# Block convolution of an S4 and SwiGLU stack: one sum of each unit as an accumulating transfer, and the kernel's first spectra read from DRAM

## The chip, the cores and the metric

The kernel runs on one core of one Trainium2 chip. The metric is device time in microseconds (us) of one execution; the runs of the kernel before gave 1077.13, 1077.5 and 1078.07, median 1077.5. Lower is better.

Engines are named as in the profile: PE is TensorE (matmuls), DVE is VectorE, ACT is ScalarE, POOL is GpSimd and SP is SyncE, which issues most transfers. Each engine works through its own list of instructions in order, and so does each issuing queue.

## The reference, cut to what matters

The input `x` has one batch, 2048 positions and 512 channels. Two layers are applied with the same weights; each is a long convolution along the positions (S4), then a SwiGLU block, both with a layernorm ahead and a residual behind.

```python
K = jnp.einsum("dn,dnl,dn->dl", Cc, P, dB).real        # kernel of 2048 taps per channel
Kf = rfft2(pad(K));  Uf = rfft2(pad(u))                # zero-padded to 4096
y = irfft2(Uf * Kf)[:L] + u * Dskip                    # causal convolution
...
x = x + _A_ref(_layernorm(x), ...)                     # convolution
x = x + (silu(n @ w_gate) * (n @ w_up)) @ w_down       # SwiGLU, n = _layernorm(x), F = 1376
```

All of it is float32 in and out.

## The kernel before

**Blocks and pairs.** The 2048 positions are cut into four blocks of 512. A pair is (layer, block); the eight pairs are done in the order `SEQ = ((0,0),(0,1),(0,2),(1,0),(0,3),(1,1),(1,2),(1,3))`. For each pair there is a convolution (`ssm`) and a feed-forward part (`ffn`). The main loop emits the convolution of pair i+1 ahead of the feed-forward part of pair i, so that the two run beside each other.

**Convolution of a block.** A 512-position block is turned into spectra by matmuls with DFT tables (`forward`, PE line L284, results taken by ACT and DVE). The output block b is the inverse transform of a sum over k = 0..b of (spectrum of kernel block k) times (spectrum of input block b−k). It is done in eight *units* a pair: two halves h of the channels, four residues q of the frequencies (`s` counts them). Per unit and k, DVE makes one product of 128x1024 float32 (L817: all four real and imaginary combinations at once, into `yk` for k = 0, else into `t`) and for each k > 0 one sum `yk += t` (L820). Two small rows (L825, L826, 128x256) then fold `yk` into a complex result, further sums (L772, L773, L838 to L850) make the four inputs of the inverse transform, and PE does the inverse (`pi`, L789), six matmuls of 128x256 for each.

The kernel's spectra are in DRAM (`wdr`, blocks k = 1 to 3), and those of k = 0 stay in SBUF for the whole run (`w0r`, 16 KB a partition). A product with k > 0 loads its two factors by SP: `w` (L813) and `uu` (L815), 256 KB each, three buffers of each kind. `yk` and `t` have one buffer each.

**Feed-forward part.** It is done in two halves of 256 positions a pair, 16 in all. In each half PE makes six groups of gate and up products in PSUM, `pgu`, which has two buffers: five whole groups (L935, L936, L938, 48 matmuls each) and one *remainder* of 96 columns (L904 to L906), which comes first. ACT takes the gate through Silu (L941), DVE multiplies with the up product (`sg`, L942; L913 for the remainder), ACT and DVE split the result in two float16 parts (`hh` L943, `hl` L944), and PE multiplies these with `w_down` (`py`, L951 to L953, 66 matmuls of 128x512). A group of PE can start only when DVE's `sg` row of the group two before it has read its buffer. Weights and activations are split in high and low float16 parts, which is why every product has three matmuls.

**What sets the order.** Until about 340 us the order is written out by hand. From there a scheduler places the instructions of all engines by priority: feed-forward rows on ACT and DVE, and the DFT matmuls, carry a high priority (`BOOST`), convolution rows on DVE carry none. The scheduler's order is fixed when the kernel is built: on the chip an engine doesn't overtake a row that waits.

**POOL** has little work here: it stores spectra to DRAM (`udr`, L744), and makes the inverse square roots of the norms (`rs`, L231), on which the next half's input depends.

Of the kernel before, what the change touches and what calls it, by code (L numbers as in the profile page):

```python
# [11 lines left out]
F32 = mybir.dt.float32  # L12
# [4 lines left out]
OP = mybir.AluOpType  # L17
# [5 lines left out]
P = 128  # L23
# [9 lines left out]
DC = 64  # L33
# [44 lines left out]
def kernel(ctx, tc, x, a_re, a_im, b_re, b_im, c_re, c_im, log_dt, d_skip,  # L78
# [7 lines left out]


    BUFS = dict(ga=1, gb=1, n=1, bt=1, z=1, u=3, y1=1, uu=3, w=3, t=1, bd=2, t1=3,
                xf=1, nn=1, hh=1, hl=1, sg=1, hf=1, stats=2, stats2=2, ef=1)

    def tl(shape, name, tag, dt=F32):
        return sb.tile(shape, dt, name=name, tag=tag, bufs=BUFS[tag])
# [40 lines left out]
    w0r = sb.tile([P, 2, 4, NQ, 2, DC], F32, name="w0r")  # L133
# [620 lines left out]
    def ssm_half(layer, b, h):  # L754
        first = layer == 0 and b == 0
        half = SEQ.index((layer, b)) >= INV
        hs = slice(h * HD, (h + 1) * HD)
        free = iv[h] if first else iv[0]

        def slot():  # L760
            return free.pop(0) if free else tl([P, 2, HD], "yf", "w")

        def done(t):
            if any(t is o for o in ivs):
                free.append(t)
        if half and not yl2:
            yl2.append(tl([P, 2, 2, 2, HD], "yl2", "hf", F16))

        def add_sub(x, y):

            t = slot()
            V.tensor_tensor(t, x, y, OP.add)  # L772
            V.tensor_tensor(x, x, y, OP.subtract)  # L773
            done(y)
            return t, x

        def inverse(pi, r, v):

            if half:
                yl = yl2[0][:, r % 2]  # L780
                A.activation(yl[:, 0], v, AF.Copy, scale=sy[:, 0:1])
                stt(yl[:, 1], v, sy[:, 0:1], yl[:, 0], OP.subtract)
            with tc.high_priority(offset=0 if first else BOOST):
                if half:
                    terms = [(eih[:, r, i, le], yl[:, ly, i]) for i in range(2) for le, ly in ((0, 0), (0, 1), (1, 0))]
                else:
                    terms = [(ei[:, r, i], v[:, i]) for i in range(2)]
                for k, (e, o) in enumerate(terms):
                    PE.matmul(pi[:, r % 2], lhsT=e, rhs=o, start=k == 0, stop=k == len(terms) - 1)  # L789
# [12 lines left out]
        for s in range(4):  # L802
            hq, q, u = ahead.pop(0)
            nxt = next(spec, None)
            if nxt:
                ahead.append(nxt)
            yk = tl([P, NQ, 2, 2, DC], "yk", "y1")
            for k in range(b + 1):
                if k == 0:
                    w, uu = w0r[:, h, q], spectrum(u) if any(u is o for o in fss) else u  # L810
                else:
                    w = tl([P, NQ, 2, DC], "w", "w")
                    nc.sync.dma_start(w, wdr[k, h, q])  # L813
                    uu = tl([P, NQ, 2, DC], "uu", "uu")
                    nc.sync.dma_start(uu, udr[layer][b - k, h, q])  # L815
                t = tl([P, NQ, 2, 2, DC], "t", "t") if k else yk
                V.tensor_tensor(t, uu.unsqueeze(2).to_broadcast([P, NQ, 2, 2, DC]),  # L817
                                w.unsqueeze(3).to_broadcast([P, NQ, 2, 2, DC]), OP.mult)
                if k:
                    V.tensor_tensor(yk, yk, t, OP.add)  # L820
            if any(u is o for o in fss):
                fs.append(u)
            y = slot()
            yo = whole(y)
            V.tensor_tensor(yo[:, 0], yk[:, :, 0, 0], yk[:, :, 1, 1], OP.subtract)  # L825
            V.tensor_tensor(yo[:, 1], yk[:, :, 0, 1], yk[:, :, 1, 0], OP.add)  # L826
# [24 lines left out]
        done(d_)  # L851
        inverse(pj, 3, b_)
        result(pi, 0)
        yield
        result(pj, 2)
        yield
# [123 lines left out]
    with tc.manual_schedule(engines={mybir.EngineType.Activation, mybir.EngineType.DVE, mybir.EngineType.PE, mybir.EngineType.Pool}):  # L980
# [168 lines left out]


        c, kts = NCH - 1, (kt2[:, 0], kt2[:, 1])
        xs, eh, yl2 = [None] * 3, [], []
# [159 lines left out]
```

## Time and profile before

| | us |
|---|---|
| median of three runs | 1077.5 |
| the profiled execution, time | 1077.3 |
| the profiled execution, span from first to last instruction | 1075.0 |
| PE busy, DVE busy, ACT busy, POOL busy | 1015.1, 966.5, 544.4, 103.9 |
| the 96 sums L820, the 96 products into `t` L817 | 117.5, 117.5 |

Around the span lie 2.3 us. In the views, "busy" of an engine is the share of a stretch in which at least one instruction was in flight, "mean ns" the length of one instruction. Instructions of one engine overlap a little at their ends, so the step from one start to the next is what an instruction costs a full engine. A matmul record of 128x256 is 0.27 us long while the next one starts 0.11 us later.

A row of a timeline or a chain gives the start, the length, the engine and line, output and inputs; in brackets stands idle time before it and what ended it ("0.55 <-DVE sg L942").

### The profile page before, as it was taken

Reading aid. Unit: us, or ns where it says so; the run is one execution under the profiler, and the core shown is the slowest. Engines: PE = TensorE matmul, PEld = TensorE weight load, DVE = VectorE, ACT = ScalarE, POOL = GpSimd, SP = SyncE. Lnnn points to the kernel's source line nnn. Section 1 sums busy time; section 2 is a strip of 40 time slices with the busy share of each in tenths; the row PEclk is TensorE's granted clock in tenths of the full one; section 3 lists DMA queues with packets and bytes.
Section 4 is the critical chain, followed back from the end, with each engine's and each line's share of the span. In section 5 each row is a group of like instructions: output and inputs, shape, how many; then the busy total and the mean of one; then the engine's idle time right before and its main releaser. Section 6 shows DMA issues by size and latency. Waiting matters only on the chain.

```text
span 1075.0 us, 22004 instructions
## 1 busy us (share of the span) xinstructions
PE 1015.1 (94%) x8918; PEld 801.8 (75%) x8918; DVE 966.5 (90%) x1405; ACT 544.4 (51%) x1093; POOL 103.9 (10%) x163
## 2 busy tenths in 40 slices
PE   1979999998789999999999999999999999999998
PEld 0868888887677787777868677786868677696774
DVE  8999999999999999999999999999999999983221
ACT  6979888853268264366652235523525442144210
POOL 1112222210000001011000001101000000000000
PEclk9989999998899999999999999999999999999999
DMA  5266777878665444323054463442444244413000
GB/s 215 100 177 180 171 165 182 188 187 270 218 207 160 122 130 151 128 94 70 16 138 140 126 212 112 124 133 100 123 120 121 86 122 139 126 36 64 1 26 20
DMA packets 120104, 139.74 MB, mean 130 GB/s; under 512 B 50609, under 2 KB 75697, under 8 KB 119234
## 3 DMA queue, kind: packets, MB, share of 16 engines
q1 hardware_dynamic: 108098, 112.83, 34.9%
q0 software_dynamic: 11904, 25.50, 10.2%
q8 instruction: 70, 1.15, 0.5%
q14 instruction: 32, 0.26, 0.1%
HBM read 91.36 MB, written 30.67 MB: 114 GB/s over the span
## 4 chain that ended last, share of the span: by engine, by line
DVE 37%; PE 27%; issue 4%; DMA 3%; ACT 3%; POOL 1%; DVEq 0%; SPq 0%; ACTq 0%; POOLq 0%
DVE t L817 5%; PE pgu L938 5%; PE pgu L935 5%; PE pgu L936 5%; DVE yk L820 5%; DVE yk L817 4%; PE py L951 3%; PE py L952 3%; PE py L953 3%; DVE sg L942 2%; DVE yl L236 2%; DVE hl L944 2%; DMA st<-in_B_w_down_dram 1%; PE pi L789 1%; PE pw L550 1%
## 5 line engine op out<-in xcount | busy, mean ns | idle before, releaser
L935 PE MATMUL pgu<-mix,wall 128*128 128x256 f16 x1280 | 299.0, 273 | 5.8 <-DVE sy L629 2.1
L936 PE MATMUL pgu<-mix,wall 128*128 128x256 f16 x1280 | 298.9, 273 | 0.0
L938 PE MATMUL pgu<-mix,wall 128*128 128x256 f16 x1280 | 195.7, 273 | 0.0
L936 PEld LDWEIGHTS <-wall 128*128 128x128 f16 x1280 | 125.2, 98 | 22.6 <-issue 7.0
L935 PEld LDWEIGHTS <-wall 128*128 128x128 f16 x1280 | 125.2, 98 | 16.4 <-issue 0.9
L938 PEld LDWEIGHTS <-wall 128*128 128x128 f16 x1280 | 125.2, 98 | 14.6
L951 PE MATMUL py<-wall,hh 128*128 128x512 f16 (+1 forms) x352 | 133.4, 379 | 0.0
L952 PE MATMUL py<-wall,hh 128*128 128x512 f16 (+1 forms) x352 | 133.4, 379 | 0.0
L953 PE MATMUL py<-wall,hl 128*128 128x512 f16 (+1 forms) x352 | 132.2, 379 | 0.0
L820 DVE TENSOR_TENSOR yk<-yk,t 128x1024 f32<-128x1024 f32 x96 | 117.5, 1224 | 0.5
L817 DVE TENSOR_TENSOR t<-uu,w 128x1024 f32<-128x1024 f32 x96 | 117.5, 1224 | 0.2
L943 ACT ACTIVATE hh<-sg 128x512 f16<-128x512 f32 x80 | 50.2, 627 | 117.4 <-DVE sg L942 117.3
L942 DVE SCALAR_TENSOR_TENSOR sg<-pgu,sc,sg 128x512 f32<-128x512 f32 x80 | 60.0, 750 | 39.2 <-ACT sg L941 39.2
L550 PE MATMUL pw<-kt,ek 128*128 128x256 f32 (+1 forms) x384 | 93.4, 381 | 0.0
L941 ACT ACTIVATE sg<-pgu,sc 128x512 f32<-128x512 f32 x80 | 54.3, 678 | 75.1 <-PE pgu L938 62.1
L550 PEld LDWEIGHTS pw<-kt,ek 128*128 128x128 f32 x384 | 75.0, 199 | 8.4
L944 DVE TENSOR_TENSOR hl<-sg,hh 128x512 f16<-128x512 f32 x80 | 55.3, 691 | 8.7 <-ACT hh L943 8.6
L953 PEld LDWEIGHTS <-hl 128*128 128x128 f16 (+1 forms) x352 | 34.3, 98 | 38.0
L952 PEld LDWEIGHTS <-hh 128*128 128x128 f16 (+1 forms) x352 | 34.4, 98 | 37.7
L951 PEld LDWEIGHTS <-hh 128*128 128x128 f16 (+1 forms) x352 | 34.4, 98 | 37.3
L515 PE MATMUL pk<-wall,g 128*32 128x64 f32 x1024 | 57.4, 288 | 4.9 <-DMA g<-g 3.7
L516 PE MATMUL pk<-wall,g 128*32 128x64 f32 x1024 | 57.8, 287 | 0.7 <-issue 0.7
(276 smaller groups left out, 1930.6 us busy)
## 6 DMA issues: line engine op xcount, KB each, us to landing
uu<-udr SPq DMA_DIRECT2D x96, 256.0 KB, 3.0
w<-wdr SPq DMA_DIRECT2D x96, 256.0 KB, 2.7
g<-g POOLq DMA_DIRECT2D x6, 1024.0 KB, 9.1
udr<-fu POOLq DMA_DIRECT2D x22, 256.0 KB, 3.2
udr<-u SPq DMA_DIRECT2D x16, 256.0 KB, 3.3
kdr<-ks SPq DMA_DIRECT2D x6, 512.0 KB, 3.1
kt<-kdr SPq DMA_DIRECT2D x24, 128.0 KB, 3.0
out_dram<-xg SPq DMA_DIRECT2D x12, 256.0 KB, 2.3
```

What stands on the lines that cost most here:

```text
L516: PE.matmul(o, lhsT=g[:, 1, :, d], rhs=im[:, 0:64, d], start=False, stop=True, tile_position=(0, 32 * grp))
L550: PE.matmul(pw[:, i], lhsT=e, rhs=kt[:, :, c + 4 * k0:4 * k1:4, :].rearrange("p g k d -> p k g d"), start=c == 0, stop=c == 3)
L817: V.tensor_tensor(t, uu.unsqueeze(2).to_broadcast([P, NQ, 2, 2, DC]), w.unsqueeze(3).to_broadcast([P, NQ, 2, 2, DC]), OP.mult)
L820: V.tensor_tensor(yk, yk, t, OP.add)
L935: PE.matmul(o, lhsT=wgu(wi, k, 0)[:, fs], rhs=nh[:, k], start=k == 0, stop=False)
L936: PE.matmul(o, lhsT=wgu(wi, k, 1)[:, fs], rhs=nh[:, k], start=False, stop=False)
L938: PE.matmul(o, lhsT=wgu(wi, k, 0)[:, fs], rhs=nlo[:, k], start=False, stop=k == 3)
L942: V.scalar_tensor_tensor(sg, pgu[:, 1], sc6[:, 4:5], sg, OP.mult, OP.mult)
L944: V.tensor_tensor(hl[:, f0:f0 + 2], sg, hh[:, f0:f0 + 2], OP.subtract)
L951: PE.matmul(py[r], lhsT=hh[:n, f, rc], rhs=wd(f, 0)[:n], start=f == 0, stop=False)
L952: PE.matmul(py[r], lhsT=hh[:n, f, rc], rhs=wd(f, 1)[:n], start=False, stop=False)
L953: PE.matmul(py[r], lhsT=hl[:n, f, rc], rhs=wd(f, 0)[:n], start=False, stop=f == FT - 1)
```

## The change

From the fourth pair of `SEQ` on (`APART = 3`), two things differ.

1. **Spectra.** When the fourth pair's convolution is emitted, the spectra of k = 0 are stored from `w0r` to `wdr[0]` (one store of 2 MB, SP). From then on a product with k = 0 loads its factor `w` by SP as the others do. The 16 KB a partition of `w0r` become four more buffers of 4 KB: two for `yk`, two for `t`, three of each in all, used in turn.
2. **The sum for k = 1.** In a unit with b > 0 the product of k = 1 is no longer added by DVE: POOL issues a transfer from `t` to `yk`, within SBUF, which accumulates (128x1024 float32, 512 KB). The products of k = 2 and 3 are added to one another on DVE, and their sum to `yk`. So a unit has one DVE sum less; the very last unit of the run keeps the old form. That makes 31 transfers: eight in each of the pairs (0,3), (1,1), (1,2), seven in (1,3). The fourth pair itself, (1,0), has b = 0 and no sum at all.

```diff
+APART = 3
+        apart = SEQ.index((layer, b)) >= APART
+        if apart and not more:
+            nc.sync.dma_start(wdr[0]..., w0r...)
+            m = tl([P, 4, NQ, 2, 2, DC], "more", "w0r")
+            more.extend(itertools.cycle(o) for o in ((None, m[:, 0], m[:, 1]), (None, m[:, 2], m[:, 3])))
+            def factors(k):
+                if k == 0 and not apart:
+                    return w0r[:, h, q], spectrum(u) if any(u is o for o in fss) else u
+                w = tl([P, NQ, 2, DC], "w", "w")
+                nc.sync.dma_start(w, wdr[k, h, q])
...
+            yk = ybuf()
+            product(yk, 0)
+            behind = apart and b > 0 and not ((layer, b) == SEQ[-1] and h == 1 and s == 3)
+            if behind:
+                t = tbuf()
+                product(t, 1)
+                G.dma_start(flat(yk), flat(t), accum_op=OP.add)
+            t = None
+            for k in range(2 if behind else 1, b + 1):
+                o = tbuf()
+                product(o, k)
+                if behind and t is not None:
+                    V.tensor_tensor(t, t, o, OP.add)
+                elif behind:
+                    t = o
                 else:
+                    V.tensor_tensor(yk, yk, o, OP.add)
+            if t is not None:
+                V.tensor_tensor(yk, yk, t, OP.add)
```

In the changed kernel the product is L840, the sums are L855 and L861, the transfer is L849, the folding rows are L866 and L867, the `sg` rows L983 and (remainder) L954, the `hl` row L985, the store L772, the loads `w` and `uu` L831 and L835; `more` is the tile with the four new buffers. Up to the convolution of the fourth pair the lists of PE and DVE are the same as before; behind it the scheduler has placed everything anew.

**SP's list, at about 275 us.** The store is emitted with the fourth pair, but the scheduler has it much earlier, in the hand-ordered stage. `udr` and `uu` are input spectra, `wall` and `st` pieces of the feed-forward weights. Before:

```order
L320 DMA udr_114<-u 128x512
L815 DMA uu<-udr_114 128x512
L671 DMA wall<-in_B_w_gate_dram 128x4x344
L813 DMA w<-wdr 128x512 x2
L671 DMA wall<-in_B_w_up_dram 128x4x344
L813 DMA w<-wdr 128x512
L697 DMA st_2982<-in_B_w_down_dram 128x4x512
```

Now:

```order
L321 DMA udr_114<-u 128x512
L772 DMA wdr<-w0r 128x8x512
L835 DMA uu<-udr_114 128x512
L672 DMA wall<-in_B_w_gate_dram 128x4x344
L831 DMA w<-wdr 128x512 x2
L672 DMA wall<-in_B_w_up_dram 128x4x344
L831 DMA w<-wdr 128x512
L698 DMA st_2982<-in_B_w_down_dram 128x4x512
```

One row is new, the store, ahead of three loads of spectra and three of weights.

**DVE's list, from the tenth remainder to the first whole group behind it.** This is the second half of the feed-forward part of pair (0,3); beside it run convolution units of pair (1,2). `sg` rows belong to the feed-forward part, `nn`, `nt` and `xf` to norms and residual; rows of 128x1024 are products (with `w`) and sums of the convolution. Before, from one `sg` row to the next:

```order
L913 SCALAR_TENSOR_TENSOR sg_3015<-pgu,sc_92,sg_3015 128x192
L236 SCALAR_TENSOR_TENSOR fbt<-pf,fbt 128x512
L890 TENSOR_TENSOR nn_2990<-nn_2990,nt_2991 128x512
L817 TENSOR_TENSOR t<-uu,w 128x1024
L236 SCALAR_TENSOR_TENSOR fu<-pf,fbt 128x512
L915 TENSOR_TENSOR sg_3015<-sg_3015 128x2x96
L820 TENSOR_TENSOR yk<-yk,t 128x1024
L236 SCALAR_TENSOR_TENSOR fbt<-pf,fbt 128x512
L292 TENSOR_TENSOR fu<-fbt,fu 128x2x4x64
L942 SCALAR_TENSOR_TENSOR sg_3015<-pgu,sc_92,sg_3015 128x512
```

Now, the last twelve of the 19 rows from the remainder's `sg` row (L954) to the group's:

```order
L866 TENSOR_TENSOR bb<-more 128x256
L867 TENSOR_TENSOR bb<-more 128x256
L999 SCALAR_TENSOR_TENSOR xf<-py,sc_92,xf 128x512
L956 TENSOR_TENSOR sg_3015<-sg_3015 128x2x96
L999 SCALAR_TENSOR_TENSOR xf<-py,sc_92,xf 128x512
L840 TENSOR_TENSOR more<-uu,w 128x1024
L931 TENSOR_TENSOR nt_2991<-nn_2990 128x512
L237 SCALAR_TENSOR_TENSOR yl_3994<-bb,sy,yl_3994 128x512
L866 TENSOR_TENSOR bb<-more 128x256
L867 TENSOR_TENSOR bb<-more 128x256
L861 TENSOR_TENSOR yk<-yk,t 128x1024
L983 SCALAR_TENSOR_TENSOR sg_3015<-pgu,sc_92,sg_3015 128x512
```

Between the two `sg` rows stood eight rows, two of them 128x1024; now there are 17, four of them 128x1024 (two in the rows left out), and folding rows of two units.

**POOL's list, at the first transfers.** Now:

```order
L232 TENSOR_TENSOR rs<-mv,mhalf 128x4
L849 DMA more<-t 128x1024
L849 DMA yk<-t 128x1024
L232 TENSOR_TENSOR rs<-mv,mhalf 128x2
L849 DMA more<-t 128x1024
L952 MEMSET sg_3015 128x4x32
L849 DMA more<-t 128x1024
L232 TENSOR_TENSOR rs<-mv,mhalf 128x2
```

Before, the same stretch has only the `rs` rows and the memsets. Each transfer waits for its product on DVE, and an `rs` row that stands behind waits with it.

More of the change, by code (lines that the diff above doesn't have):

```diff
@@ L88 @@
     BUFS = dict(ga=1, gb=1, n=1, bt=1, z=1, u=3, y1=1, uu=3, w=3, t=1, bd=2, t1=3,
-                xf=1, nn=1, hh=1, hl=1, sg=1, hf=1, stats=2, stats2=2, ef=1)
+                xf=1, nn=1, hh=1, hl=1, sg=1, hf=1, stats=2, stats2=2, ef=1, w0r=1)
     def tl(shape, name, tag, dt=F32):
@@ L132 @@
     nc.sync.dma_start(x1, x[0, T:2 * T, :].rearrange("(c p) d -> p c d", p=P))
-    w0r = sb.tile([P, 2, 4, NQ, 2, DC], F32, name="w0r")
+    w0r = tl([P, 2, 4, NQ, 2, DC], "w0r", "w0r")
     sc6 = sb.tile([P, 6], F32, name="sc6")
@@ L767, in ssm_half, with buf, ybuf, tbuf @@
             yl2.append(tl([P, 2, 2, 2, HD], "yl2", "hf", F16))
+        apart = SEQ.index((layer, b)) >= APART
+        if apart and not more:
+            nc.sync.dma_start(wdr[0].rearrange("h q p c i d -> p (h q) (c i d)"), w0r.rearrange("p h q c i d -> p (h q) (c i d)"))
+            m = tl([P, 4, NQ, 2, 2, DC], "more", "w0r")
+            more.extend(itertools.cycle(o) for o in ((None, m[:, 0], m[:, 1]), (None, m[:, 2], m[:, 3])))
+        def buf(i, name, tag):
+            o = next(more[i]) if more else None
+            return tl([P, NQ, 2, 2, DC], name, tag) if o is None else o
+        def ybuf():
+            return buf(0, "yk", "y1")
+        def tbuf():
+            return buf(1, "t", "t")
+        def flat(t):
+            return t.rearrange("p c a i d -> p (c a i d)")
         def add_sub(x, y):
@@ L806, in ssm_half, with product @@
                 ahead.append(nxt)
-            yk = tl([P, NQ, 2, 2, DC], "yk", "y1")
-            for k in range(b + 1):
-                if k == 0:
-                    w, uu = w0r[:, h, q], spectrum(u) if any(u is o for o in fss) else u
-                else:
[L812 to L820, printed above, removed]
+            def factors(k):
[3 more added lines that the diff above has]
+                nc.sync.dma_start(w, wdr[k, h, q])
+                if k == 0:
+                    return w, spectrum(u) if any(u is o for o in fss) else u
+                uu = tl([P, NQ, 2, DC], "uu", "uu")
+                nc.sync.dma_start(uu, udr[layer][b - k, h, q])
+                return w, uu
+            def product(o, k):
+                w, uu = factors(k)
+                V.tensor_tensor(o, uu.unsqueeze(2).to_broadcast([P, NQ, 2, 2, DC]),
+                                w.unsqueeze(3).to_broadcast([P, NQ, 2, 2, DC]), OP.mult)
+            yk = ybuf()
[13 more added lines that the diff above has]
+                    t = o
+                else:
+                    V.tensor_tensor(yk, yk, o, OP.add)
+            if t is not None:
+                V.tensor_tensor(yk, yk, t, OP.add)
             if any(u is o for o in fss):
@@ L1151 @@
         c, kts = NCH - 1, (kt2[:, 0], kt2[:, 1])
-        xs, eh, yl2 = [None] * 3, [], []
+        xs, eh, yl2, more = [None] * 3, [], [], []
         spec, ahead = inputs(), []
```

## The prediction

> **What bounds the kernel now.** I read the busy times first, then the starts of single matmuls, then stretches of the run, and last who waited for whom.
>
> ```profile
> PE 1015.1 (94%) x8918; PEld 801.8 (75%) x8918; DVE 966.5 (90%) x1405; ACT 544.4 (51%) x1093; POOL 103.9 (10%) x163
> ```
>
> Two engines are nearly full. Whether PE is full in earnest is seen from starts, not from busy time. The timeline of PE near the end, where DVE has little to do, gives the pace that PE has by itself:
>
> ```profile
> 999.76 0.27 PE L935 MATMUL pgu<-mix,wall 128*128 128x256 f16 x1
> 999.87 0.27 PE L936 MATMUL pgu<-mix,wall 128*128 128x256 f16 x1
> 1000.41 0.27 PE L935 MATMUL pgu<-mix,wall 128*128 128x256 f16 x1
> 1000.52 0.27 PE L936 MATMUL pgu<-mix,wall 128*128 128x256 f16 x1
> ```
>
> One 128x256 matmul starts every 0.11 us. The windows (us; busy of PE, PEld, DVE, ACT, POOL with counts, granted clock, DMA share, GB/s) show both engines full up to 960, then PE alone:
>
> ```profile
> 340.00:520.80 180.80, 179.85 (x1404) 136.61 (x1403) 178.95 (x286) 92.84 (x190) 19.06 (x29) 1.00 0.37 110
> 520.80:768.50 247.70, 245.81 (x1955) 189.25 (x1954) 243.90 (x356) 105.89 (x201) 18.21 (x26) 1.00 0.42 125
> 768.50:960.00 191.50, 190.38 (x1507) 145.78 (x1507) 188.18 (x264) 66.50 (x120) 6.93 (x11) 1.00 0.39 114
> 960.00:1075.00 115.00, 110.36 (x830) 80.12 (x827) 29.53 (x45) 30.75 (x57) 1.80 (x4) 0.99 0.11 26
> ```
>
> PE keeps its pace from 340 us to the end but for a few stops. The waits of PE between 418 and 960 us (total, times, longest):
>
> ```profile
> PE pgu L935 <- DVE sg L913: 1.6, 2, 0.9
> PE pgu L935 <- DVE sg L942: 1.0, 2, 0.5
> PE pi L789 <- ACT yl L781: 0.7, 1, 0.7
> PE pf L284 <- ACT fbt L285: 0.6, 1, 0.6
> ```
>
> That is 3.9 us, each stop behind DVE or behind ACT that had waited for DVE. So the time from 340 us on is PE's own work plus what DVE makes PE wait, and a change to DVE can win no more than these 3.9 us. What it can lose has no such end: a group of PE starts only when DVE has come to the `sg` row of the group two before, and in DVE's fixed list every row ahead of it counts.
>
> **The sums that go.** 31 sums leave DVE, at the price of these rows:
>
> ```profile
> 763.28 1.22 DVE L817 TENSOR_TENSOR t<-uu,w 128x1024 f32<-128x1024 f32 x1
> 764.41 0.69 DVE L236 SCALAR_TENSOR_TENSOR fu<-pf,fbt 128x512 f32<-128x512 f32 x1
> 765.01 0.35 DVE L915 TENSOR_TENSOR sg<-sg 128x192 f16<-128x192 f32 x1
> 765.28 1.22 DVE L820 TENSOR_TENSOR yk<-yk,t 128x1024 f32<-128x1024 f32 x1
> 766.41 0.69 DVE L236 SCALAR_TENSOR_TENSOR fbt<-pf,fbt 128x512 f32<-128x512 f32 x1
> 767.01 0.69 DVE L292 TENSOR_TENSOR fu<-fbt,fu 128x512 f32<-128x512 f32 x1
> 767.61 0.75 DVE L942 SCALAR_TENSOR_TENSOR sg<-pgu,sc,sg 128x512 f32<-128x512 f32 x1
> 768.27 0.42 DVE L825 TENSOR_TENSOR mix<-yk 128x256 f32<-128x256 f32 x1
> 768.61 0.42 DVE L826 TENSOR_TENSOR mix<-yk 128x256 f32<-128x256 f32 x1
> ```
>
> From start to start: a product or sum of 128x1024 takes 1.13, a row of 128x512 0.60, `sg` 0.66, a row of 128x256 0.34. 31 sums are 35 us of DVE. By itself that would end all stops of PE.
>
> **The new order.** But the scheduler did not leave the rest where it was. I counted the rows of both lists between two fixed places of the feed-forward part: from the fifth remainder's `sg` row (520.8 us before; up to there both lists hold the same work within 0.1 us) to the first whole `sg` row behind the tenth remainder, which before is the row at 767.61 above. The feed-forward work between them is the same. The convolution rows aren't: products 67 instead of 56, sums 23 instead of 38, rows of 128x256 13 more, of 128x512 12 more (one of them as 128x2x4x64), of 128x4x64 (256 elements) 4 more. The convolution of pair (1,2) has 20 of its 24 products done there instead of 8: it runs ahead. Priced: 11 x 1.13 = 12.4, less 15 x 1.13 = 17.0, plus 13 x 0.34 = 4.4, 12 x 0.60 = 7.2, 4 x 0.34 = 1.4, in all 8.4 us *more* on DVE ahead of this row, though 15 sums have gone. PE has 19 more `pi` matmuls there, 19 x 0.11 = 2.1 us.
>
> It counts because PE stood waiting at this very place:
>
> ```profile
> 768.42 0.27 PE L935 MATMUL pgu<-mix,wall 128*128 128x256 f16 x1 [0.55 <-DVE sg L942]
> 774.75 0.27 PE L935 MATMUL pgu<-mix,wall 128*128 128x256 f16 x1 [0.50 <-DVE sg L942]
> 809.67 0.27 PE L935 MATMUL pgu<-mix,wall 128*128 128x256 f16 x1 [0.62 <-DVE sg L913]
> ```
>
> The matmul at 768.42 moves 8.4 us back, and PE has done 2.1 us of its later work by then: 6.3 us. Behind it DVE's list is light (from it to the next remainder it holds some 13 us less than before, while PE's work there is less by only those 2.1), so the stops at 774.75 and 809.67 go: less 1.1. DVE's idle time counts too: in 520.80:768.50 it was 247.7 − 243.9 = 3.8 us. A DVE that is late finds its inputs ready, but waits for POOL's `rs` and for loads can stay; bounds 0 and 3.8, I take half back, 1.9. Sum so far: 6.3 − 1.1 − 1.9 = +3.3.
>
> **The store.** It waits for the last write of `w0r`, near 276 us, and stands in SP's list ahead of loads that are wanted soon:
>
> ```profile
> L596 ACT ACTIVATE w0r<-pw x4: 277/330/386, 262.8 to 276.0; 128x128 f32<-128x128 f32 x2, 128x256 f32<-128x256 f32 x2
> 265.00:270.00 5.00, 5.00 (x26) 4.54 (x26) 3.70 (x7) 1.61 (x2) 0.00 (x0) 0.70 0.98 380
> 276.50:289.20 12.70, 9.19 (x38) 7.16 (x36) 11.17 (x21) 2.80 (x6) 0.02 (x1) 0.87 0.69 221
> 289.23 5.63 DMA st<-in_B_w_down_dram
> ```
>
> The last row is from the chain that ended last. 2.1 MB at the 380 GB/s that the full engines moved take 5.5 us of all of them; free between 276.5 and 289.2 are 0.31 x 12.7 = 3.9. So 1.6 us may be left when the weight load at 289.23 starts, and that load is on the chain. Bounds: 0 if it fits in the gaps, 5.5 if nothing does; I take 1.6. The queue itself waits little: the row ahead of the store was issued at 274.8.
>
> **The transfers.** No row shows an accumulating transfer of 512 KB within SBUF. The nearest are the same kind with 1024 KB and a plain store of 256 KB from POOL, issue to landing, and POOL's time for one issue:
>
> ```profile
> g<-g POOLq DMA_DIRECT2D x6, 1024.0 KB, 9.1
> udr<-fu POOLq DMA_DIRECT2D x22, 256.0 KB, 3.2
> L495 POOL DMA_DIRECT2D g<-g x6: 1231/1240/1261, 72.3 to 209.2; - x6
> w<-wdr SPq DMA_DIRECT2D x96, 256.0 KB, 2.7
> ```
>
> A line between the two gives 5.2 us. In DVE's new list the rows between a unit's last product and the first row that needs its transfer are worth 8 us or more in pair (0,3), but 6.0, 5.3, 6.2 and 5.0 us in the first four units of (1,1). At 5.2 DVE waits 0.2 us in all; at 9.1 about 8 (a wait in one unit lengthens the time for the next); at half of 9.1 nothing. I take 0.5. On POOL, `rs` rows and stores of `udr` stand behind transfers that wait for DVE; what DVE then wants from `rs` stands behind those products in its own list, so the wait itself costs nothing and the issue at most 1.2 us each time; it is in the half of idle time that I kept. The 40 loads more of `w` (k = 0) have three buffers as before and 2.7 us of landing against 3 to 4 products' time; no cost, and if that cover fails, it comes on top of DVE's lateness.
>
> **Sum.** +3.3 + 1.6 + 0.5 = +5.4 on the profiled execution's 1077.3, so 1082.7; the median of the runs lies 0.2 above that execution: 1082.9. About 2.2 us (0.2%) is what a measurement of this kernel can tell from no change.
>
> **The rivals.**
>
> *DVE's relief wins* (faster). If DVE runs more freely than my count says, because the rows it does early are done in time that was idle or would be lost to waits, nothing holds PE and the 3.9 us of stops go: 1077.3 − 3.9 + 0 to 1.6 = 1073.4 to 1075.0. For it: 35 us off a list that is 98% busy in the stretch. Against it: the place where DVE decides comes behind more than 20 of the 31 transfers, and the rows ahead of it have grown. It decides where the 8.4 falls under 2.1 + 3.9. The Trainium skill (Perfetto Trace Analysis, "Identifying the Most-Contended Engine") judges TensorE by the busy time of its weight loads rather than of its matmuls; by that rule PE, with 75%, has room and DVE, with 90%, is the engine to relieve, which is this rival. The trace doesn't bear it out: starts every 0.11 us are PE's full pace here. Chance 0.14.
>
> *The two cancel.* All 3.8 us of idle time are filled and the store fits: 1077.3 + 6.3 − 1.1 − 3.8 = 1078.7, or less if PE's two buffers take up some. Chance 0.19.
>
> *Late transfers* (slower still). If a transfer takes nearer to 9.1 us, DVE waits up to 8 us more ahead of the deciding row: 1086 to 1091. Against it: the landing of the six 1024 KB ones was steady, beside a DVE as full as here (their landing, and the window of one of them):
>
> ```profile
> DMA to landing us min/median/max: 8.9/9.1/9.2
> 150.00:200.00 50.00, 47.27 (x663) 41.48 (x662) 49.30 (x62) 43.64 (x85) 14.53 (x21) 0.97 0.80 182
> ```
>
> The Trainium skill (SBUF — State Buffer, "SBUF: two separate sides") warns that a DVE operation that holds the port it shares with GpSimd keeps GpSimd from writing the descriptors of its transfers; by that rule they would start late beside a full DVE. The steady 9.1 us show nothing of it. Chance 0.12.
>
> My forecast, slower by 2.5 to 8 us through the order, has 0.55.
>
> **Numbers.** Faster by over 0.2%: the first rival, 0.14. Within 0.2%: the second, 0.19, less a little that ends beyond, 0.17. Slower: 0.69. The range reaches from 1076.0, which takes in nearly all of the second rival, to 1089.5, most of the late transfers; it leaves out the first rival and the worst of the last, 0.2 together.
>
> **What would show it.** Right: PE waits for DVE `sg` rows (L983, L954) or `yl` grow from 3.9 to some 8 to 12 us, nearly all before the eleventh remainder; from there PE has no stop, and DVE idles for long. DVE's busy time falls by some 35 us in spite of a longer run. Landing of L849 near 5 us. The first feed-forward stage starts 0 to 3 us later than before. Wrong: if PE's stops before 770 us don't grow, the count of rows misled me; if the first half of the feed-forward stage already starts over 4 us late, the store is the cause; if DVE waits long for the transfers, their landing is.

## The result and the profile after

The changed kernel takes 1117.72 us (median of 4 runs, 1113.68 to 1121.05): 1.0371 times the kernel before, 95% interval 1.0325 to 1.0417, or 40.2 us slower. The prediction was 1082.9 with a range to 1089.5: the sign was right, the size wrong by a factor of seven. The profiled execution is the fastest of the four, 36.4 us above that of the kernel before; the views below add up to this figure, not to 40.2.

The busy times (engine, us, share of the span, instructions) and four stretches of the changed kernel, with the same columns as in the windows of the prediction; last, the first of these stretches (520 to 930 us) in the kernel before:

```profile
PE 1028.5 (92%) x8918; PEld 806.2 (73%) x8918; DVE 932.8 (84%) x1374; ACT 544.8 (49%) x1093; POOL 141.2 (13%) x194
```

```profile
520.00:930.00 410.00, 382.38 (x2926) 287.56 (x2924) 355.97 (x530) 159.52 (x302) 57.71 (x65) 0.97 0.70 178
735.00:743.00 8.00, 8.00 (x75) 7.17 (x74) 6.63 (x11) 2.18 (x6) 1.63 (x2) 1.00 1.06 251
743.50:750.50 7.00, 0.55 (x6) 0.35 (x4) 5.49 (x8) 2.55 (x5) 0.00 (x0) 0.68 1.14 290
751.00:754.50 3.50, 3.50 (x17) 2.24 (x16) 3.50 (x5) 0.39 (x1) 0.67 (x1) 0.50 0.87 214
```

```profile
520.00:930.00 410.00, 406.99 (x3234) 313.29 (x3233) 403.33 (x581) 167.16 (x311) 25.72 (x36) 1.00 0.41 123
```

DVE is 33.7 us less busy, as the missing sums say. Yet in 520 to 930 us PE now stands idle for 27.6 us instead of 3.0, DVE for 54.0 instead of 6.7, and the DMA engines' share has risen from 0.41 to 0.70. Both compute engines wait: the loss isn't work. (The share adds up the times of all packets, so it can pass 1.)

Where it arises is read from the 16 remainder `sg` rows of DVE (L913 before, L954 after), one for each half of the feed-forward part; after less before, us:

| half | 1 to 5 | 6 | 7 | 8 | 9 | 10 | 11 | 12 | 13 | 14 to 16 |
|---|---|---|---|---|---|---|---|---|---|---|
| changed kernel | −2.1 to −0.7 | −0.8 | 8.1 | 17.7 | 19.8 | 24.5 | 25.0 | 32.9 | 37.5 | 37.4 to 38.5 |

So the store of 2 MB shows no cost: the feed-forward part starts 1.2 us earlier. All is lost between 568 and 945 us of the kernel before, behind the first transfers (from 533 us on in the changed kernel). What PE waited for longest in 520 to 930 us (total, times, longest), and landings in the same stretch (KB, median us from issue to landing), of the changed kernel:

```profile
PE pgu L976 <- DVE sg L954: 7.5, 3, 3.7
PE pf L285 <- ACT fbt L286: 6.7, 2, 6.5
PE pi L809 <- DVE yl L237: 5.7, 4, 3.2
PE pgu L976 <- DVE sg L983: 3.6, 5, 1.7
```

```profile
w<-wdr SPq DMA_DIRECT2D x94, 256.0 KB, 3.3
uu<-udr SPq DMA_DIRECT2D x63, 256.0 KB, 3.6
more<-t POOLq DMA_DIRECT2D x14, 512.0 KB, 6.5
more<-more POOLq DMA_DIRECT2D x6, 512.0 KB, 6.2
mix<-nn SPq DMA_TRANSPOSE x22, 3.7
hl<-sg SPq DMA_TRANSPOSE x16, 3.7
```

In the kernel before, `w` and `uu` land in 2.7 and 3.0 there, `mix<-nn` in 2.5, and:

```profile
hl<-sg SPq DMA_TRANSPOSE x18, 2.3
```

The longest stop shows how a late landing reaches PE. The chain of the changed kernel through it (start, us, what):

```profile
740.34 0.24 PE pf L285 x3
740.58 7.10 DMA hl<-sg
747.92 0.69 ACT sg L982
748.61 0.71 ACT nn L928
749.34 0.63 ACT nn L930
749.97 0.49 ACT fbt L286
750.50 1.44 PE pf L285 x6
751.94 0.21 PE pgu L976
752.16 0.21 PE pgu L977
```

A transposing load out of `sg`, 2.3 us in the median before, takes 7.1 here, with the DMA engines' share above 1 in the windows around it and a transfer that adds in flight from 739.4 to 747.5 us. ACT, idle for 10.0 us by then, writes `sg` again only when it has landed, what stands behind on ACT is late with it, and PE gets no `fbt`. The last two rows start 0.22 us apart, not 0.11: PE comes out of the stop at half pace, and the window from 751 us has a granted clock of 0.50. The same rows in run e10 below, whose transfers copy and don't add: the two loads out of `sg` have landed 7.2 us after the first was issued instead of 8.6, and PE stands for 3.2 us instead of 6.5. So a copy delays them too, and adding delays them more.

### The profile page after: what moved, and what is told of

The parts are those of the page before. It is cut to its first block, busy times and chain, and to the rows that moved or that the text cites. A ratio compares the mean times of both kernels' runs of the same rounds, so it can differ in the third digit from the quotient of the medians.

```text
span 1111.9 us, 22102 instructions
## 1 busy us (share of the span) xinstructions
PE 1028.5 (92%) x8918; PEld 806.2 (73%) x8918; DVE 932.8 (84%) x1374; ACT 544.8 (49%) x1093; POOL 141.2 (13%) x194
## 4 chain that ended last, share of the span: by engine, by line
DVE 27%; PE 23%; DMA 11%; issue 7%; ACT 4%; POOL 1%; SPq 1%; DVEq 0%; POOLq 0%; ACTq 0%
PE pgu L976 5%; PE pgu L977 5%; PE pgu L979 5%; DVE more L840 3%; DVE t L840 3%; DMA w<-wdr 3%; PE py L992 2%; PE py L993 2%; PE py L994 2%; DVE yk L840 2%; DVE sg L983 2%; DVE hl L985 2%; DMA more<-t 2%; DVE yk L859 2%; DVE yl L237 1%
## 5 line engine op out<-in xcount | busy, mean ns | idle before, releaser
L976 PE MATMUL pgu<-mix,wall 128*128 128x256 f16 x1280 | 303.4, 275 | 15.1 <-DVE sg L954 7.5
L977 PE MATMUL pgu<-mix,wall 128*128 128x256 f16 x1280 | 303.4, 275 | 0.0
L979 PE MATMUL pgu<-mix,wall 128*128 128x256 f16 x1280 | 198.8, 275 | 0.0
L983 DVE SCALAR_TENSOR_TENSOR sg<-pgu,sc,sg 128x512 f32<-128x512 f32 x80 | 60.1, 752 | 61.4 <-ACT sg L982 61.4
L840 DVE TENSOR_TENSOR more<-uu,w 128x1024 f32<-128x1024 f32 x48 | 58.7, 1222 | 10.9 <-DMA uu<-udr 6.2
L985 DVE TENSOR_TENSOR hl<-sg,hh 128x512 f16<-128x512 f32 x80 | 55.2, 690 | 11.1 <-ACT hh L984 11.1
L993 PEld LDWEIGHTS <-hh 128*128 128x128 f16 (+1 forms) x352 | 34.6, 98 | 37.5 <-issue 0.3
L516 PE MATMUL pk<-wall,g 128*32 128x64 f32 x1024 | 57.8, 288 | 4.2 <-DMA g<-g 4.2
L232 POOL TENSOR_TENSOR rs<-mv,mhalf 128x2 f32<-128x2 f32 (+1 forms) x21 | 38.1, 1815 | 183.6 <-ACT mv L231 145.5
L840 DVE TENSOR_TENSOR t<-uu,w 128x1024 f32<-128x1024 f32 x48 | 58.9, 1227 | 0.7 <-DMA w<-wdr 0.7
```

Of the source, the lines that this page charges most:

```text
L516: PE.matmul(o, lhsT=g[:, 0, :, d], rhs=re[:, 0:64, d], start=True, stop=False, tile_position=(0, 32 * grp))
L840: V.tensor_tensor(o, uu.unsqueeze(2).to_broadcast([P, NQ, 2, 2, DC]), w.unsqueeze(3).to_broadcast([P, NQ, 2, 2, DC]), OP.mult)
L976: PE.matmul(o, lhsT=wgu(wi, k, 0)[:, fs], rhs=nh[:, k], start=k == 0, stop=False)
L977: PE.matmul(o, lhsT=wgu(wi, k, 1)[:, fs], rhs=nh[:, k], start=False, stop=False)
L979: PE.matmul(o, lhsT=wgu(wi, k, 0)[:, fs], rhs=nlo[:, k], start=False, stop=k == 3)
L983: V.scalar_tensor_tensor(sg, pgu[:, 1], sc6[:, 4:5], sg, OP.mult, OP.mult)
```

## The experiments

Three theories stood at the start. **O**, the prediction's own: the new order of DVE's list puts products ahead of rows that PE needs. **D**: the transfers load the DMA engines, and other transfers land late. **W**: the 40 more `w` loads hold up SP's list and its three buffers. Later expectations call O "theory B", and T the cost of a transfer. (In the changed kernel `yk` and `t` have three tiles each; where an expectation speaks of two buffers or second tiles, these are meant.) "Above before" is the difference to the median of the kernel before on the same chip. Many runs leave a product or a sum out of the output, or take another factor: they price time alone.

| run | us | above before | ratio, 95% interval |
|---|---|---|---|
| e1 no transfer | 1091.39 | 14.3 | 1.0130 (1.0115 to 1.0145) |
| e2 loads only | 1089.77 | 12.7 | 1.0123 (1.0105 to 1.0140) |
| e3 an eighth | 1087.05 | 10.0 | 1.0087 (1.0070 to 1.0104) |
| e4 no w loads | 1101.13 | 24.1 | 1.0217 (1.0199 to 1.0234) |
| e5 buffers only | 1093.65 | 17.7 | 1.0163 (1.0144 to 1.0183) |
| e6 sums gone | 1085.42 | 9.5 | 1.0082 (1.0063 to 1.0102) |
| e7 store instead | 1085.67 | 9.7 | 1.0090 (1.0075 to 1.0105) |
| e8 own buffers | 1077.85 | 1.9 | 1.0015 (1.0005 to 1.0024) |
| e9 transfers alone | 1126.87 | 50.3 | 1.0470 (1.0455 to 1.0486) |
| e10 plain copy | 1094.96 | 18.4 | 1.0177 (1.0156 to 1.0198) |
| e11 double store | 1093.14 | 16.6 | 1.0160 (1.0134 to 1.0186) |
| e12 relief alone | 1075.64 | −0.9 | 0.9983 (0.9969 to 0.9997) |
| e13 store and copy | 1097.30 | 20.4 | 1.0195 (1.0164 to 1.0226) |
| e14 add in DRAM | 1107.00 | 30.1 | 1.0282 (1.0241 to 1.0322) |
| e15 half add | 1094.62 | 17.7 | 1.0169 (1.0152 to 1.0186) |
| e16 one yk | 1126.12 | 49.2 | 1.0463 (1.0431 to 1.0496) |
| e17 add aside | 1102.66 | 26.3 | 1.0243 (1.0227 to 1.0260) |
| e18 add, two yk | 1114.37 | 38.0 | 1.0343 (1.0322 to 1.0365) |

### Which part: transfers, loads, or what is left

```diff
 e1  -                G.dma_start(flat(yk), flat(t), accum_op=OP.add)
 e2  -            behind = apart and b > 0 and not (...)
     +            behind = False
 e3  +                G.dma_start(flat(yk)[:, :128], flat(t)[:, :128], accum_op=OP.add)
 e4  +                if k == 0: return uu, uu            # ahead of the load of w
```

> The changed kernel with its 31 accumulating transfers left out (the first product of each unit is never added to the second, so the output lacks one product; 31 sums have left DVE and nothing has taken them over). The order of DVE's list, the 40 additional w loads and the 2 MB store are as in the changed kernel. Theory D (the DMA engines' load by the transfers, some 90 us of all 16 engines, makes the w, u and transposing loads land later and so stops PE): 1072 to 1080 us, the remainder rows of the 7th to 13th FFN stage back at the times of the kernel before, DMA share of 520 to 930 us near 0.5. Theory O (the order of DVE's list: products brought ahead of the rows that PE needs, as my prediction had it): nothing in the order changes, so 1110 us or more. Theory W (the 40 more w loads in SP's one queue and three w buffers): 1105 us or more.

> The changed kernel with all sums back on DVE: no transfers, but the 2 MB store, the 40 additional w loads and the two buffers for each of the products as in the changed kernel. Theory D: 1075 to 1083 us, since the 10 MB of loads are about a third of the additional traffic. Theory O: 1076 to 1079 us, for DVE's list is that of the kernel before. Theory W: 1100 us or more, with the losses at the same remainder rows as in the changed kernel.

> The changed kernel with each accumulating transfer cut to the first eighth of its columns (64 KB instead of 512 KB; seven eighths of one product are left out of the output). Issue on POOL, waits and order stay; the traffic of the transfers goes down to an eighth. Theory D: 1073 to 1083 us, landings near 2.5 us, hl<-sg and mix<-nn landings back near 2.3 to 2.7 us. Theory O and theory W: 1105 us or more. A fourth theory, P (what costs is the wait of DVE and POOL's rows on the transfers, whatever their size): 1095 to 1110 us.

> The changed kernel without the 40 additional w loads: in their place the first product of a unit multiplies u's spectra by themselves (so this product's values are others, its operation and size are the same). The 31 transfers, their waits and DVE's order stay. Theory D: 1100 to 1115 us, for three quarters of the additional traffic remain. Theory O: 1110 us or more. Theory W: 1073 to 1083 us.

Only e4 came out as one theory had it (D, 1100 to 1115 us). Without transfers 26 of the 40 us go (D in part), yet 14.3 stay, and the landings of `w` and `hl<-sg` are then 2.9 and 2.3 us, hardly later than before. Without the `w` loads 24.1 stay. e2 has every sum on DVE and no transfer, and still loses 12.7: nothing that I had in the sum. An eighth of each transfer (e3) costs nothing over none, though it keeps every issue and every dependence: theory P of its expectation falls too.

### What the remaining 13 us are

```diff
 e5  e4's edit and  behind = False
 e6  e4's edit and  no G.dma_start
 e7  +                G.dma_start(sdr[next(sn)], flat(t))     # 31 places in DRAM
 e8  behind = False, yk and t one tile each, and
     +                w = tl([P, NQ, 2, DC], "w", "w") if k else next(more[0])   # 8 tiles
```

> Neither the 40 additional w loads nor the transfers: the first product of a unit multiplies u's spectra by themselves (other values, same operation), all sums stand on DVE; the 2 MB store and the two buffers for each of the products stay as in the changed kernel. It is the zero for the two costs that the first four runs showed apart (loads alone +12.5, transfers alone +24). Theory D: 1076 to 1079 us, so that the loads' traffic is the whole of +12.5. If the store or the buffers' order cost something of their own: 1082 us or more.

> As the run before it in this list, with 31 sums gone from DVE and nothing in their place (one product is left out of the output): the order of DVE's list is that of the changed kernel, with no additional traffic but the store. It prices DVE's relief and the order by themselves. Theory D, with a relief worth the few stops that PE had: 1072 to 1076 us. Theory O (products brought ahead): 1081 us or more.

> The changed kernel with each accumulating transfer replaced by a plain transfer of the same 512 KB from the second product's tile to a part of DRAM that nobody reads (the sum is left out of the output): same queue, same issue on POOL, but no row of DVE waits for it except for the use of the tile again. If the traffic itself does the harm (theory D): 1105 to 1118 us, or 14 us above the kernel before plus a part of the transfers' 26 us by the share of the engines' time that q0 shows. If DVE's waits for the sum (9.3 us of them) do it (theory P): 1090 to 1094 us, as without transfers.

> The kernel with all sums on DVE and the 40 additional w loads (1089.8 us), but the loads of the first product get eight buffers of their own (yk and t have one each, as in the kernel before) instead of taking turns in the three w buffers. Same traffic. Theory D (traffic): 1087 to 1092 us. Theory W in its narrow form (the turn in three buffers makes the loads start late and hold up what stands behind them in SP's list): 1076 to 1081 us.

e5 and e8 settle it. e5 has neither loads nor transfers nor a sum less, only the store and three tiles for `yk` and `t`, and is 17.7 us above before. e8 has the store and all 40 loads, but one tile each: 1.9. So the loads and the store cost next to nothing by themselves; it is the tiles. (e8 gives the loads buffers of their own as well, and W in its narrow form had foreseen its time. It is e5, which has none of these loads and still loses, that decides against W as the cause here.) In e8 DVE's list holds its products and sums at every `sg` row exactly where the kernel before has them. In e5 up to 9 products and 6 sums more stand ahead of the same `sg` rows, as a scheduler would have it that fills DVE with convolution rows as soon as a tile is free. DVE's timeline of e5 between a remainder's `sg` and the next whole group's:

```profile
569.06 0.41 DVE L955 SCALAR_TENSOR_TENSOR sg<-pgu,sc,sg 128x192 f32<-128x192 f32 x1
569.39 0.68 DVE L792 TENSOR_TENSOR mix<-bb,mix 128x512 f32<-128x512 f32 x1
...
573.18 1.21 DVE L860 TENSOR_TENSOR more<-more 128x1024 f32<-128x1024 f32 x1
574.31 1.21 DVE L841 TENSOR_TENSOR more<-uu,w 128x1024 f32<-128x1024 f32 x1
575.45 1.22 DVE L860 TENSOR_TENSOR more<-more,t 128x1024 f32<-128x1024 f32 x1
576.58 0.35 DVE L957 TENSOR_TENSOR sg<-sg 128x192 f16<-128x192 f32 x1
576.85 0.68 DVE L793 TENSOR_TENSOR bb<-bb,mix 128x512 f32<-128x512 f32 x1
577.45 1.21 DVE L841 TENSOR_TENSOR yk<-fbt 128x1024 f32<-128x1024 f32 x1
578.59 0.74 DVE L984 SCALAR_TENSOR_TENSOR sg<-pgu,sc,sg 128x512 f32<-128x512 f32 x1
```

and PE's at its end:

```profile
579.38 0.37 PE L977 MATMUL pgu<-mix,wall 128*128 128x256 f16 x1 [4.25 <-DVE sg L984]
```

From `sg` to `sg` DVE, never idle, takes 9.53 us, 569.06 to 578.59. In the kernel before the same two rows stand 4.13 us apart, and PE does not wait:

```profile
568.23 0.41 DVE L913 SCALAR_TENSOR_TENSOR sg<-pgu,sc,sg 128x192 f32<-128x192 f32 x1
572.36 0.74 DVE L942 SCALAR_TENSOR_TENSOR sg<-pgu,sc,sg 128x512 f32<-128x512 f32 x1
```

So O names the right mechanism, but its origin is the tiles. With 31 sums gone on top (e6) 9.5 remain: the relief, with another order of the list, gives back 8.

e7, with the loads, moves 512 KB for each sum and comes out below e1 (9.7 against 14.3) and below both forecasts, 1090 us or more: no harm shows of a plain transfer that nobody waits for.

### The transfer by itself

```diff
 e9  before, with the transfer; later products:  V.tensor_tensor(yk, yk, o, OP.add)
 e10 +                G.dma_start(flat(yk), flat(t))
 e11 +                G.dma_start(sdr[next(sn)], flat(t).unsqueeze(1).to_broadcast([P, 2, NQ * 4 * DC]))
 e12 before, with 31 sums left out
```

> The kernel before with the 31 accumulating transfers alone: w0r stays in SBUF, no additional w loads, no store, and one tile each for yk and t as before (the later products are summed into yk behind the transfer). Through the list of DVE's rows the products stand at most 3 ahead of the kernel before, against 14 in the changed kernel. Theory B (the second tiles let the products be listed ahead of the rows that PE needs, +13 to +17 us by the runs with buffers alone) and T (each accumulating transfer costs on top, +16 to +26): here T stays and B is gone, 1090 to 1103 us. If the loss of the transfers comes only with the order of B: 1075 to 1085 us. If DVE's direct wait for the one tile rules (31 landings of 6.5 us less what is covered): above 1110 us.

> The changed kernel, whose transfers copy the second product over the first instead of adding it (the first product is left out of the output). Every list of every engine is row for row that of the changed kernel; only the kind of the transfer differs. If the adding makes the cost (it reads both sides: 2.9 us of all 16 engines for each, against 1.4 for the plain store of the same size): 1090 to 1100 us with landings near 5 us. If the dependence of DVE on the landing makes it, whatever the kind: 1110 us or more.

> As the run with plain stores of 512 KB to DRAM that no row waits for (1085.7 us), each now of 1024 KB (the tile twice), so that the DMA engines' time is about that of the accumulating transfers, and t is held as long or longer. The sum is left out of the output. If the traffic alone does the harm: 1105 to 1118 us. If not: 1084 to 1092 us, and what the transfers cost in the changed kernel then lies in DVE's waits for them.

> The kernel before without the 31 sums and with nothing in their place (one product is left out of the output): no transfers, no additional loads, one tile each. It is the most that the change could have won. The products stand up to 11 ahead of the kernel before in DVE's list, 14 to 17 sums fewer. Forecast of the prediction's first rival: 1073 to 1075 us. Theory B says the advance of the products takes it back: 1076 to 1083 us.

e12 is the ceiling, between its two forecasts: 0.9 us, were the sums free. (Its products stand up to 11 ahead of the kernel before, but products and sums together at most 1; in e5, together, it is up to 14.) e9, 50.3 above before, shows the other way to pay. With one `t`, DVE has to wait for the landing before the next product (DVE's waits in e9: total, times, longest):

```profile
DVE t L836 <- DMA yk<-t: 53.0, 21, 7.2
```

e10 has every engine's list row for row as in the changed kernel, and only doesn't add: 18.4 instead of 40.2. So 22 us hang on the adding: what it takes of the engines, and DVE's waits for the sum, 9.3 us instead of 2.0. What adding does to the engines is read from the landings (min, median, max) of the 31 transfers and from the queue's packets, MB and share, of the changed kernel and of e10:

```profile
DMA to landing us min/median/max: 4.7/6.5/9.9
q0 software_dynamic: 16368, 41.75, 18.0%
```

```profile
DMA to landing us min/median/max: 3.0/5.2/7.2
q0 software_dynamic: 16368, 41.75, 14.1%
```

The same packets and bytes. Less the share of the kernel before (10.2% of its span), a transfer that adds keeps all 16 engines busy for 2.9 us, one that copies for 1.4. But e11, with the engines' time of the adding (q0 17.7%), is only 2.3 above e1, and 6.9 above e7, which stores half as much. Engine time alone isn't it either. (By its expectation the rest would then lie in DVE's waits; e14, below, has none and is slower still.)

### Adding, and waiting for it

```diff
 e13 +                G.dma_start(sdr[next(sn)], flat(t))
     +                G.dma_start(flat(yk), flat(t))
 e14 +                G.dma_start(sdr[next(sn)], flat(t), accum_op=OP.add)    # 4 places, set once
 e15 +                G.dma_start(flat(yk)[:, :512], flat(t)[:, :512], accum_op=OP.add)
 e16 more: yk (None,), t (None, m[:, 2], m[:, 3]); 4 tiles of m for w with k = 0
```

> The changed kernel with, in place of each accumulating transfer, two plain ones of 512 KB in a row on the same queue: the second product to a part of DRAM that nobody reads, then the same tile over the first product (the first product is left out of the output). Traffic as with the double stores (1093.1 us, no row waits for them), and DVE waits for the second, which should land after 6.5 to 7 us, with no adding anywhere. If the late landing makes the cost of the transfers: 1108 to 1125 us. If the adding does: 1093 to 1099 us, as with the plain copy or the double store.

> The changed kernel, whose transfers add the second product to a part of DRAM (set once from w0r by 2 MB more of store) instead of to the first product, so that no row of DVE waits for the sum but by the use of the tile again; the sum is left out of the output. If the adding's traffic harms the other loads: 1105 us or more. If it is the wait for the landing: 1085 to 1097 us.

> The changed kernel with half of the columns in each accumulating transfer (256 KB; the other half of one product is left out of the output). By the wait for the landing, with the runs of 64 KB (3.7 us, +10 us) and of the plain copy (5.0 us, +18 us) as its neighbours: landings near 4.8 us and 1090 to 1097 us. If the adding itself costs by its bytes, half of 26 us over the 1091.4 us without transfers: 1102 to 1107 us.

> The changed kernel with its transfers, but one tile for the first product, three for the later ones, and four buffers of their own for the first product's w loads. In DVE's list products and sums together then stand at most 3 rows ahead of the kernel before up to the tenth FFN stage, where the changed kernel has up to 6. If the order (theory B) and the transfers add up: 1100 to 1108 us. If the transfers' wait does more harm with one tile, as it did with single tiles throughout (1126.9 us): 1118 us or more.

e13 did not make what it was for: its copies landed after 3.8, 6.0 and 7.9 us (min, median, max) and DVE waited 1.2 us for them in all, so it tells little of a late landing. e14 speaks for the adding: 30.1 though no row waits for the sum, with `hl<-sg` at 4.2 us and `mix<-nn` at 5.3 (medians of 520 to 990 us). Its zero is e7, which stores where e14 adds: the lists of PE, ACT, DVE and POOL are the same row for row but for two rows of DVE near 300 us, and SP has one store more near 278 us. Up to the fifth remainder e14 is 0.2 us behind e7, at the fourteenth 22.5. The landings of the 31 transfers and DVE's largest wait for loads of `w` in 520 to 930 us (total, times, longest), of e7, then of e14:

```profile
DMA to landing us min/median/max: 3.0/5.0/6.3
DVE more L842 <- DMA w<-wdr: 7.3, 6, 3.6
```

```profile
DMA to landing us min/median/max: 5.3/7.5/8.9
DVE more L843 <- DMA w<-wdr: 19.7, 7, 4.9
```

In neither does DVE wait for one of these transfers. So adding in DRAM instead of storing costs 20.4 us though nobody waits for it: the landings that are waited for are those of others, of `w` above all. e15, half the bytes, costs as much as the plain copy, where the wait theory had put it: size counts more than in proportion. e16 came out by its second forecast, 1118 us or more: with one `yk` DVE waits 60.0 us for transfers directly. Fewer tiles let fewer rows run ahead and buy the wait. The last pair parts adding and waiting inside SBUF, with the same tiles:

```diff
 both more: yk (None, m[:, 0]), t as in the changed kernel
 e17 +                G.dma_start(flat(m[:, 1]), flat(t), accum_op=OP.add)
```

> The changed kernel with two tiles for the first product instead of three; the third is zeroed once, and each transfer adds the second product to it instead of to the first (the sum is left out of the output), so that no row waits for the landing but by the use of the tile again. If the adding's work in the DMA engines delays other transfers and that is the cost: 1100 to 1112 us, as when it adds in DRAM. If DVE's wait for the sum is the cost: 1087 to 1096 us.

> The same two tiles for the first product, but the transfers add to it as in the changed kernel, so that DVE waits for the sum. Both theories: 1112 to 1125 us; the difference to the run that adds aside is the price of the wait, 8 to 15 us by the adding theory, 20 us or more by the wait theory.

26.3 and 38.0. The adding costs 12.0 more than no transfer (e1) with nobody waiting, and the wait 11.7 more, though the lists of these three runs differ (below). The landings of e17 and e18, and DVE's waits for transfers in e18:

```profile
DMA to landing us min/median/max: 4.5/6.0/11.7
```

```profile
DMA to landing us min/median/max: 4.6/6.2/11.0
DVE yk L861 <- DMA yk<-more: 4.3, 2, 4.1
DVE bb L866 <- DMA more<-more: 3.9, 1, 3.9
DVE mix L866 <- DMA more<-t: 2.1, 1, 2.1
DVE bb L866 <- DMA yk<-t: 1.6, 1, 1.6
```

With three smaller ones 14.3 us: few waits, the longest 4.1 us. In these two runs and the changed kernel the medians are 6.0 to 6.5, but the latest land after 9.9 to 11.7 us; those of the plain transfers (e7, e10, e11, e13) after 6.3 to 8.6.

## Why the prediction was wrong, point by point

**The bound.** Right. PE paces the run and a change to DVE can win little: I said 3.9 us at most, e12 won 0.9. Of the signs that I named, DVE's busy time (33.7 less of the 35 foreseen) held; the feed-forward part started 1.2 us earlier, not 0 to 3 later; PE's stops grew to several times the 8 to 12 us, and went on behind the eleventh remainder (25.0 us lost there, 38.5 at the fourteenth); L849 landed after 6.5 instead of 5.

**The order.** The mechanism was right, the size a third of it: +6.3 in one place less 3.0 of relief, +3.3 net, against 9.5 in e6 (tiles and relief alone, in a list of its own). I priced the one place that decided before, and took it that DVE's lighter list behind it would need no more stops. The tiles let products run ahead through halves 6 to 12, and PE stopped at several of them (e5's at 575, 769, 776, 786, 885 us). The rule of the Trainium skill behind the first rival (Perfetto Trace Analysis, "Identifying the Most-Contended Engine"), relieve the busiest engine, is answered by e12: 35 us less DVE work, 0.9 us.

**The store.** 1.6 was foreseen, 0 found; e8 has store and loads together at 1.9.

**The `w` loads.** "No cost; if that cover fails, it comes on top". By themselves that held (e8). On top of the tiles' order the runs differ by 4.8 (e1 less e6), which is within what another list does (below), on top of the transfers too by some 16 (the changed kernel less e4). That the cover fails when the engines are full would fit, but isn't shown.

**The transfers.** This is the step that failed: "I take 0.5". With the lists of the changed kernel, the adding alone is worth 21.8 us (the changed kernel less e10). The landing of 5.2 us by a line between two rows is what e9 (median 5.0) and the plain copy (5.2) have; the changed kernel had 6.5. The time to the first use, 5.0 to 6.2 us in (1,1), was short enough to matter: DVE waited 9.3 us in all, 6.1 of them there, more than the 8 that I had put to a landing of 9.1. But the larger error was to price a transfer only through its own landing. I did not ask what 2.9 us of all engines for each of 31 transfers does to those beside it. The row that I quoted beside the six steady `g<-g` transfers has a share of 0.80 at 182 GB/s, while the store's row has 380 GB/s at 0.98: I read it as steadiness under load, and not as the warning that something in that window fills the engines with half the bytes.

**The rival of late transfers** was the nearest to the truth, had 0.12, and reached only to 1091.

**The sum as measured**, each step a pair of runs: tiles and order with the relief 9.5 (e6), loads 4.8 (e1), adding 12.0 (e17), waiting 11.7 (e18), and 2.2 more with the third `yk` tile. The steps aren't independent: by the order of the pairs the loads are worth 4.8 or 16. And at each step the scheduler places everything anew: between the runs of these pairs 191 to 420 of DVE's 1374 rows stand elsewhere in the list. What that alone can do shows where less to do took longer: e1, without transfers, is 4.3 above e3 with an eighth of each, and e5, without the loads, 5.0 above e2 with them. So a step of 5 us is not shown to be what it is called. Two pairs have the same lists, and on them the main reading rests: 21.8 us for adding instead of copying (the changed kernel and e10) and 20.4 for adding instead of storing (e14 and e7). How the 21.8 part into harm to other transfers and DVE's own waits is shown only roughly, by e17 and e18.

**What stays open:** why plain transfers of nearly the same engine time (e11, 2.7 us each) harm the others so much less than adding ones (e14, e17), though `mix<-nn` is late in all three (4.2, 5.3 and 3.5 us). What differs is DVE's wait for `w` in 520 to 930 us: 6.4, 21.6 and 13.5 us. A run with a steady late landing and no adding was tried (e13) and did not get it.

## What to carry to other kernels

Before work is moved to the DMA engines, price what it takes of all 16 of them and whose landings share them, not only its own landing. More buffers are not free under a scheduler that fills an engine greedily: compare how many rows stand ahead of those that the bounding engine waits for. And measure the ceiling first, by leaving the work out (e12): here it was 0.9 us. Last, compare runs whose lists are the same: a scheduler that places everything anew moved these times by some 5 us by itself.

## What the runs showed of the hardware

- **Adding inside SBUF** holds the engines twice as long as copying the same bytes (2.9 against 1.4 us of all 16 for 512 KB) and lands 1.3 us later in the median. While these transfers were in flight, a packet of 4 KB in POOL's queue took 328 ns in the median (the changed kernel, e17, e18; e14, into DRAM, the same), and 159 ns where they copy or store (e7, e10, e11).
- **A transposing load in flight beside adding transfers** took 4.8 us in the median and up to 10.4 in 520 to 930 us of the changed kernel; the others there took 2.5 in the median, as in the kernel before (2.4, up to 5.7). Beside plain copies (e10) it was 4.1 and 8.8; and e1, without any transfer, has one of 7.4.
- **PE at half pace after a stop.** After the stop of 6.6 us at 743.8, 21 matmuls started at double distance under the clock of 0.50 shown above. From 340 us on 89 starts were so, which cost 10.0 us. Counted as what each distance of starts has beyond the median for its shape, PE lost 44.2 us there (before: 6.0, and no start at double distance): a quarter of the additional loss is not waiting itself but what a long stop leaves behind. The Trainium skill (TensorE: Matmul & The Clock Gate, "Part 1: The HAM clock gate (the "warmup" mystery)") has the clock halved after an idle window of about 3.4 us that runs freely. The traces agree roughly: all stops of 3.8 us or more, here and in e1, e5, e11, e14, e17 and e18, were followed by it; of those of 2.3 to 3.5 us some were (2.48 at 630.3 in the changed kernel) and some not (3.33 at 525.9). A stop of 2.48 us is shorter than that window, so the page's figure alone doesn't explain it.
